# A head-mixing attention with a bilinear layer behind it: loads moved at two places, and the first chunk's scores spread over more PSUM banks

## Chip, core and metric

The kernel runs on one core of one Trainium2 chip. The metric is device time of one execution in microseconds (us). Most executions of this kernel agree within a few tenths of a per cent.

## What is computed

Inputs are drawn at random; q, k and w_pre are scaled by 8. The attention has 4 batches, 12 heads, 448 tokens and a head dimension of 64; the layer behind it has 1792 tokens, model width 768 and inner width 1536.

```python
scores = (1 / sqrt(64)) * q @ k.T                       # per batch and head
scores = einsum('bhij,hg->bgij', scores, w_pre)         # heads are mixed before ...
attn = exp(scores - max(scores)); attn /= sum(attn) + 1e-9
attn = einsum('bhij,hg->bgij', attn, w_post)            # ... and after the softmax
x = (attn @ v).transpose(0, 2, 1, 3).reshape(1792, 768)
out = ((x @ w_a) * (x @ w_b)) @ w_out
```

The weights of the layer are 64-bit numbers, which arrive as pairs of 32-bit words and are turned into float32 on the chip.

## The kernel before

**Tiling.** The queries of a batch are cut into chunks of 120, 120, 120 and 88 (16 chunks in all), and a chunk into units of 20 queries (6, 6, 6 and 5 units; 23 in a batch, 92 in all, counted from 0). Heads are kept in two groups of six, so that head i and head i + 6 make a pair.

**Steps of the attention.** `qk(c, i)` multiplies the queries of chunk c with the keys of pair i, two matmuls into a PSUM tile of two banks (tag "t", one buffer), and ScalarE copies both halves into the chunk's tile "s" (L226, L227; "s" has two buffers, so chunk c takes the place of chunk c - 2). `gather(u)` fetches a unit's rows out of "s" by four DMAs on SyncE's queue, so that head and query lie on partitions (L243, tiles "sb", buffers for four units). `premix(u)` mixes the heads by matmuls (L263, PSUM tag "m"), `smax` takes the maximum on VectorE (L272) and the exponential on ScalarE (L273), `norm` prepares the second mixing matrix on VectorE (L280 to L286), `postmix` multiplies (L296, PSUM tag "p"), `evac_p` copies the result on ScalarE (L307, tile "pt"), and `av` multiplies groups of units with v (L321, PSUM tag "x") and sends the result to DRAM (L330, L331), from where it is read as x.

**Order.** The order of all instructions is written out by hand. The loop over s runs one step for each unit: `premix(s)`, then copies of unit s - 2, `smax(s)`, the score pairs and v products that stand in a table for this step, `norm(s)`, `postmix(s - 1)`. A unit's gathers are issued three steps ahead (AH = 3). GpSimd holds loads of k, q and v for later chunks in its queue; a small copy ("tick", L121) behind each unit's sums paces them. The six pieces of v of the next batch are loaded one in each of six steps of a batch, from step V_AT on (`load_v`, L191). The six k tiles of the next batch follow between steps 12 and 16 of a batch (L195), and the first two score pairs of the next batch both stand at step 15.

**First chunk.** Ahead of the loop stand chunk 0's six pairs, 60 idle matmuls (L141), and the gathers of four units.

**Hand-over.** Once chunk 15's last score pair is placed, at step 84, the layer's first work is mixed into the last units. `load_raw` loads a weight tile of 768 KB on SyncE's queue, `load_x` one third of a batch's x, 448 KB, from DRAM (L369); x takes the buffer of chunk 14's "s". `later(fn, n)` puts an issue n steps later, ahead of that step's `premix`. `tail_ops` hands out conversions: from step 85 on, four operations at the end of each step, first six VectorE operations and one of GpSimd on the first weight (L400 to L406), then the same on the second, whose first operation (L400) is the last of step 86, then x (L375, L376). A SyncE DMA waits for the DMA eight places before it in its queue, besides its data.

Of the kernel before, what the change touches and what calls it, by code (L numbers as in the profile page):

```python
# [7 lines left out]
F32 = mybir.dt.float32  # L8
# [13 lines left out]
def talking_heads_bilinear_kernel(  # L22
# [11 lines left out]
    nc = tc.nc  # L34
    B, _, G, S = k.shape
    H, D = 2 * G, 64
# [5 lines left out]
    QG = 3  # L42
# [18 lines left out]
    WARM3 = 60  # L61
    Q1E = 3
    KL = 3
    V_AT = 9
    LQ = 4
    scale = 1.0 / float(D) ** 0.5

# [1 line left out]
    for b in range(B):  # L69
        t0 = 0  # L70
        while t0 < S:
            n = min(CHUNK, S - t0)
# [23 lines left out]
    ps = ctx.enter_context(tc.tile_pool(name="ps", bufs=2, space=PSUM))  # L96
# [28 lines left out]
    def later(fn, n=3):  # L125
        todo_at.setdefault(now[0] + n, []).append(fn)

    def setup():
        nc.vector.memset(ones, 1.0)
        nc.vector.memset(wrep, 0.0)  # L130
        for r in (0, 64):
            nc.gpsimd.dma_start(out=wrep[r:r + QH * H, 0], in_=w_pre.partition_broadcast(QH))
        for r in (0, 64):
            nc.gpsimd.dma_start(out=wrep[r:r + QH * H, 1], in_=w_post.partition_broadcast(QH))
# [8 lines left out]
    def act_table():  # L143
        nc.vector.memset(p2, 0.0)
        nc.scalar.activation(p2, p2, ACTF.Exp)
# [37 lines left out]
    kt, qraw, qt, vt = {}, {}, {}, {}  # L183
    st, sbt, mt, at, ant, ptt, pps, xps = {}, {}, {}, {}, {}, {}, {}, {}
# [8 lines left out]
    def load_k(b, i):  # L193
        t = k_p.tile([128, S], F32, tag="k", name="k")
        (nc.sync if b == 0 else nc.gpsimd).dma_start(out=t, in_=k[b, :, i])  # L195
        kt[b, i] = t
# [22 lines left out]
    def qk(c, i):  # L219
        b, t0, n = chunks[c]  # L220
        if c not in st:
            st[c] = big.tile([128, H, S], F32, tag="s", name="s")
        sp = ps.tile([128, 2, 512], F32, tag="t", name="pst", bufs=1)[:, :, :S]
        for g in range(2):
            rows = slice(D * g, D * g + D)
            nc.tensor.matmul(sp[:n, g], lhsT=qt[c, i // QG][rows, i % QG], rhs=kt[b, i][rows])  # L226
        nc.scalar.copy(st[c].rearrange("p (g i) s -> p i g s", g=2)[:n, i], sp[:n])  # L227
# [108 lines left out]
    for c in range(1, NC):  # L336
        b, t0, _ = chunks[c]
# [14 lines left out]
    for a in range(NA - 1):  # L352
        b, u0, n = groups[a]
# [11 lines left out]
    def load_x(b, parts=(0, 1, 2)):  # L365
        if b not in xt:
            xt[b] = big.tile([128, 2, KD, S], F32R, tag="s" if b < 2 else "pt", name="xhl")
        for i in parts:
            nc.sync.dma_start(out=xt[b].bitcast(F32)[:, 1, 2 * i:2 * i + 2], in_=xd[b][:, 2 * i:2 * i + 2])  # L369
# [10 lines left out]
    def load_raw(u):  # L380
        kind, i, e = u
        t = mo["c"].tile([128, CW, 2], I32, tag="raw", name="raw")
        nc.sync.dma_start(
            out=t.rearrange("p (k f) t -> p k (f t)", k=KD), in_=(w_ab if kind == "f" else w_out)[i, e].bitcast(I32)
        )
        raws[u] = t
# [106 lines left out]
    order = [("f", f, e) for f in range(3) for e in range(2)] + [("o", 0, 0), ("o", 0, 1)]  # L493
# [52 lines left out]
    with tc.manual_schedule():  # L546
        setup()
        load_q(0, 0)
        load_k(0, 0)
        load_k(0, 1)  # L550
        load_q(0, 1)
        load_k(0, 2)
        load_k(0, 3)
        act_table()
        warm_up(WARM)
        setup_mask()
        spread_q(0, 0, nc.vector)
        for i in range(G):
            if i == 1:
                spread_q(0, 1, nc.vector)  # L560
            if i + 4 < G:
                load_k(0, i + 4)
            if i == 2:
                load_q(1, 0)
                load_q(1, 1)
            qk(0, i)
        spread_q(1, 0)
        setup_w()
        nxt_g = AH + 1
        for u in range(nxt_g):  # L570
            gather(u)
        warm_up(WARM3)
        tail = iter(())

        for s in range(NU + 2):
            now[0] = s
            if s == last_prep + 1:
                open_moe()
                load_raw(order[0])
                later(lambda: load_raw(order[1]), 1)  # L580
                for i in range(3):
                    later(lambda i=i: load_x(0, (i,)), 2 + i)
                tail = tail_ops()
            if s == NU - 2:
                load_x(1)
            if s == NU - 1:
                load_x(2)
            while nxt_g <= min(s + AH, NU - 1) and ready.get(units[nxt_g][0], -1) < s:
                gather(nxt_g)
                nxt_g += 1  # L590
            pace(s - 1)
            if s in (2, 4):
                for i in range(3):
                    load_v(0, 3 * (s // 2 - 1) + i)
            b, i = divmod(s, NUB)
            if b + 1 < B and 0 <= i - V_AT < 6:
                load_v(b + 1, i - V_AT)
            for fn in todo_at.pop(s, ()):
                fn()
            if s < NU:  # L600
                premix(s)
            if s >= 2:
                for k_ in blocks_of(s - 2):
                    evac_p(k_)
            if s < NU:
                for k_ in blocks_of(s):
                    smax(k_)
            for it in items.get(s, ()):
                it[0](*it[1:])
            if s < NU:  # L610
                for k_ in blocks_of(s):
                    norm(k_)
            if 0 <= s - 1 < NU:
                for k_ in blocks_of(s - 1):
                    postmix(k_)
            for it in after.get(s, ()):
                it[0](*it[1:])
            if s >= last_prep + 2:
                take(tail, RATE if s < NU - LATE else RATE2)
            if s == NU:  # L620
                for _ in tail:
                    pass
                tail = split_ops(1)
                for k_ in blocks_of(NU - 1):
                    evac_p(k_)
                run_a(0, 0)
            if s == NU + 1:
                run_b(0, 0)
        for p in range(6):
            av(NA - 1, p)  # L630
        for t in sorted(todo_at):
            for fn in todo_at[t]:
                fn()
        todo_at.clear()
        load_x(3)
        for _ in tail:
            pass
        now[0] = 999
        late = conv_ops(range(2, 4))
        take(late, T1)  # L640
        run_a(0, 1)
        take(split_ops(2), 12)
        run_b(0, 1)
        take(late, T2)
        run_a(0, 2)
        take(late, T3)
        run_b(0, 2)
        for _ in late:
            pass
        run_a(1, 0)  # L650
        take(split_ops(3), 12)
        run_b(1, 0)
        todo = {(0, 3): order[4], (1, 1): order[5], (1, 2): order[6], (1, 3): order[7]}
        for i, u in enumerate(order[8:]):
            todo[2 + i // 3, i % 3 if u[0] == "f" else 2] = u
        nxt = 6
        pairs = [(0, 3), (1, 1), (1, 2), (1, 3)] + [(f, b) for f in range(2, KF) for b in range(B)]
        for i, (f, b) in enumerate(pairs):
            now[0] = 1000 + i
            for fn in todo_at.pop(now[0], ()):  # L660
                fn()
            if (f, b) in todo:
                ops, fin = conv(todo[f, b])
                for fn in ops:
                    fn()
                if nxt < len(order):
                    load_raw(order[nxt])
                    nxt += 1
            run_a(f, b)
            if (f, b) in todo:  # L670
                fin()
            run_b(f, b)
            if f == KF - 1 and b == 1:
                load_o(0)
                load_h(0)
                load_o(1)
                split_o(0)
            if f == KF - 1 and b > 1:
                for i in range(KF // 2 * (b - 2), KF // 2 * (b - 1)):
                    split_h(0, i)  # L680
            if b == B - 1:
                del wt["f", f]
        now[0] += 1
        for t in sorted(todo_at):
            for fn in todo_at[t]:
                fn()
        todo_at.clear()
        for j in range(B * KD):
            b, m = divmod(j, KD)
            load_o(j + 2)  # L690
            if m == 0 and b + 1 < B:
                load_h(b + 1)
            if j + 1 < B * KD:
                split_o(j + 1)
            if b + 1 < B and m >= 2:
                for f in range(3 * (m - 2), 3 * (m - 1)):
                    split_h(b + 1, f)
            run_o(j)
# [48 lines left out]
```

## Time and profile before

| | |
|---|---|
| three runs | 1010.79, 1013.9, 1014.28 us; median 1013.9 |
| profiled execution | 1010.31 us; span of its instructions 1008.6 us |
| busy share of the span | TensorE 95%, weight loads 77%, VectorE 51%, ScalarE 41%, GpSimd 29% |
| mean granted TensorE clock | 0.983 of 2.4 GHz |
| DMA | 146.6 MB moved, mean 145 GB/s |

The attention ends near 476 us of the span; the layer fills the rest and keeps TensorE busy throughout. A timeline row holds the start and the duration in us, engine, line, operation, out<-in and count; in brackets stands the idle time of the engine before it and what ended it. PE is TensorE, ACT ScalarE, DVE VectorE, POOL GpSimd, SPq the queue of SyncE.

### The profile page before, as it was taken

What the parts mean: (1) busy time and instruction counts of PE and PEld (TensorE: products, weight loads), DVE (VectorE), ACT (ScalarE), POOL (GpSimd) and SP (SyncE); (2) the same over time, 40 slices, a digit from 0 to 9 for tenths busy, and PEclk for the clock granted to TensorE, in tenths of its full rate; (3) what the DMA queues carried; (4) which work ended last, traced back from release to release, by engine and by line L of the source; (5) the groups of instructions that cost most, each with busy time, mean ns of one, the idle gap of its engine ahead of it and who ended that gap; (6) DMA issues with size and microseconds to landing.
All of it is one profiled execution on the core that took longest, in us unless ns stands there. A gap on an engine that the chain in (4) does not pass through costs nothing.

```text
span 1008.6 us, 17007 instructions
## 1 busy us (share of the span) xinstructions
PE 962.7 (95%) x6388; PEld 774.4 (77%) x6388; DVE 513.1 (51%) x1090; ACT 418.5 (41%) x854; POOL 293.0 (29%) x321
## 2 busy tenths in 40 slices
PE   7798899979999899988999999999999999999998
PEld 4465566646665566666889999999999998999997
DVE  1455355535555355567767565665555454432510
ACT  2675466756676566656321111111111133342521
POOL 2223011320123111112133323333233225555542
PEclk9999799989999899999999999999999999999999
DMA  3446233553346333348335333423333256556441
GB/s 117 156 137 199 95 123 123 156 164 97 123 136 191 104 131 119 114 155 260 112 105 188 134 118 138 146 97 139 114 139 136 85 215 244 192 202 257 146 137 68
DMA packets 63472, 146.60 MB, mean 145 GB/s; under 512 B 6252, under 2 KB 48000, under 8 KB 62368
## 3 DMA queue, kind: packets, MB, share of 16 engines
q1 hardware_dynamic: 58528, 131.11, 38.1%
q0 software_dynamic: 4864, 14.42, 5.1%
q8 instruction: 51, 0.84, 0.3%
q14 instruction: 29, 0.24, 0.1%
HBM read 80.23 MB, written 26.74 MB: 106 GB/s over the span
## 4 chain that ended last, share of the span: by engine, by line
PE 82%; DMA 11%; DVE 3%; ACT 2%; SPq 1%; issue 1%; POOL 0%; ACTq 0%; DVEq 0%
PE pp L296 13%; DMA sb<-s 10%; PE pst L226 7%; PE mp L263 7%; PE xp L321 6%; PE po L445 6%; PE po L446 6%; PE po L444 6%; PE pa L444 5%; PE pa L445 5%; PE pa L446 5%; PE pb L446 5%; PE pb L444 5%; PE pb L445 5%; ACT s L227 1%; DVE xhl L376 1%
## 5 line engine op out<-in xcount | busy, mean ns | idle before, releaser
L296 PEld LDWEIGHTS pp<-kr,a 124*112 124x112 f32 (+1 forms) x1440 | 159.7, 182 | 50.7 <-issue 33.0
L272 DVE TENSOR_REDUCE nm<-mp 124x1 f32<-124x448 f32 x180 | 104.2, 619 | 154.3 <-PE mp L263 154.3
L296 PE MATMUL pp<-kr,a 124*112 124x120 f32 (+1 forms) x1440 | 177.3, 278 | 2.8 <-ACT pt L307 1.7
L273 ACT ACTIVATE a<-mp,nm 124x448 f32<-124x448 f32 x180 | 112.7, 631 | 90.7 <-DVE nm L272 90.5
L226 PE MATMUL pst<-k,q 64*120 64x448 f32 (+1 forms) x384 | 100.1, 599 | 30.9 <-ACT s L227 30.8
L406 POOL TENSOR_TENSOR cvm<-cvm,cvr 128x768 int32<-128x768 int32 x36 | 67.0, 1860 | 211.6 <-DVE cvm L405 211.6
L434 POOL TENSOR_TENSOR wl<-rawo,wh 128x768 fp32r<-128x768 f32 x48 | 93.0, 1960 | 100.9 <-ACT wh L433 100.9
L307 ACT COPY pt<-pp 112x480 f32<-112x480 f32 x180 | 97.0, 574 | 51.7 <-PE pp L296 51.6
L456 ACT COPY sa<-pa 128x448 f32<-128x448 f32 x48 | 25.7, 536 | 221.7 <-PE pa L446 216.6
L121 POOL COPY tick<-rs 60x1 f32<-60x1 f32 x92 | 17.1, 186 | 344.9 <-DVE rs L280 344.9
L445 PE MATMUL pa<-xhl,wh 128*128 128x448 f32 x288 | 104.6, 363 | 1.9 <-DVE xhl L376 1.9
L445 PE MATMUL po<-hl,wh 128*128 128x448 f32 x288 | 104.5, 363 | 0.7 <-DVE hl L481 0.7
L444 PE MATMUL pa<-xhl,wh 128*128 128x448 f32 x288 | 104.6, 363 | 0.0
L446 PE MATMUL pa<-xhl,wl 128*128 128x448 f32 x288 | 104.4, 363 | 0.0
L444 PE MATMUL po<-hh,wh 128*128 128x448 f32 x288 | 104.4, 362 | 0.0
L446 PE MATMUL po<-hh,wl 128*128 128x448 f32 x288 | 104.4, 362 | 0.0
L446 PE MATMUL pb<-xhl,wl 128*128 128x448 f32 x282 | 102.3, 363 | 0.9 <-POOL wl L434 0.9
L226 PEld LDWEIGHTS pst<-k,q 64*120 64x120 f32 (+1 forms) x384 | 27.0, 175 | 98.5 <-ACT s L227 39.9
L444 PE MATMUL pb<-xhl,wh 128*128 128x448 f32 x282 | 102.2, 362 | 0.0
L445 PE MATMUL pb<-xhl,wh 128*128 128x448 f32 x282 | 102.2, 362 | 0.0
L227 ACT COPY s<-pst 120x896 f32<-120x896 f32 (+1 forms) x96 | 86.4, 900 | 36.6 <-PE pst L226 19.8
L263 PE MATMUL mp<-sb,wp 60*64 60x448 f32 x720 | 95.2, 564 | 3.8 <-ACT a L273 3.5
(64 smaller groups left out, 1373.1 us busy)
## 6 DMA issues: line engine op xcount, KB each, us to landing
sb<-s SPq DMA_DIRECT2D x356, 105.0 KB
raw<-in_w_ab_dram SPq DMA_DIRECT2D x24, 768.0 KB
rawo<-wod SPq DMA_DIRECT2D x24, 768.0 KB
hd<-hf SPq DMA_DIRECT2D x48, 224.0 KB
raw<-in_w_out_dram SPq DMA_DIRECT2D x12, 768.0 KB
v<-in_v_dram POOLq DMA_DIRECT2D x24, 224.0 KB, 6.0
xhl<-xd SPq DMA_DIRECT2D x12, 448.0 KB
hl<-hd SPq DMA_DIRECT2D x4, 1344.0 KB
```

What stands on the lines that cost most here:

```text
L226: nc.tensor.matmul(sp[:n, g], lhsT=qt[c, i // QG][rows, i % QG], rhs=kt[b, i][rows])
L227: nc.scalar.copy(st[c].rearrange("p (g i) s -> p i g s", g=2)[:n, i], sp[:n])
L263: nc.tensor.matmul(mt[u, i // 2][col:col + M], lhsT=wp[r:r + m, :M], rhs=tiles[i % 2][r:r + m])
L272: nc.vector.tensor_reduce(nm[:m], mp[:m], axis=AXX, op=ALU.max, negate=True)
L273: nc.scalar.activation(a[:m], mp[:m], ACTF.Exp, bias=nm[:m], scale=1.0, accum_out=rs[:m])
L296: nc.tensor.matmul(pp[:, r, :, :n], lhsT=an[:m, r * P:(r + 1) * P], rhs=kr[:m, :, :n])
L307: nc.scalar.copy(ptt[a][:P, :, :, o:o + n], pps.pop((u, j))[:, :, :, :n])
L406: lambda: nc.gpsimd.tensor_tensor(m, m, r, op=ALU.add),
L434: nc.gpsimd.tensor_tensor(ll[:, sl], raw, hh.bitcast(F32)[:, sl], op=ALU.subtract)
L444: nc.tensor.matmul(o, lhsT=hh[:, k0 + kk], rhs=mh[:, kk], start=(kk == 0), stop=False)
L445: nc.tensor.matmul(o, lhsT=hh[:, k0 + kk], rhs=ml[:, kk], start=False, stop=False)
L446: nc.tensor.matmul(o, lhsT=ll[:, k0 + kk], rhs=mh[:, kk], start=False, stop=(kk == n - 1))
```

## The change

Three edits. At the hand-over x's three parts are issued at steps 84, 85 and 87 instead of 86, 87 and 88, and the second weight at step 86 instead of 85. In chunk 0 the pairs 1, 3 and 5 no longer use the two-bank tile: each of their two halves takes a tile of one bank, of tag "m", "p" or "x", and VectorE copies it to "s". And v's pieces are loaded at steps 6 to 11 of a batch instead of 9 to 14.

```diff
-    V_AT = 9
+    V_AT = 6
...
         if c not in st:
             st[c] = big.tile([128, H, S], F32, tag="s", name="s")
+        if c == 0 and i % 2:
+            for g in range(2):
+                rows = slice(D * g, D * g + D)
+                sp = ps.tile([128, 512], F32, tag="mpx"[i // 2], name="psq")[:, :S]
+                nc.tensor.matmul(sp[:n], lhsT=qt[c, i // QG][rows, i % QG], rhs=kt[b, i][rows])
+                nc.vector.tensor_copy(st[c][:n, g * G + i], sp[:n])
+            return
         sp = ps.tile([128, 2, 512], F32, tag="t", name="pst", bufs=1)[:, :, :S]
...
                 load_raw(order[0])
-                later(lambda: load_raw(order[1]), 1)
-                for i in range(3):
-                    later(lambda i=i: load_x(0, (i,)), 2 + i)
+                load_x(0, (0,))
+                later(lambda: load_x(0, (1,)), 1)
+                later(lambda: load_raw(order[1]), 2)
+                later(lambda: load_x(0, (2,)), 3)
                 tail = tail_ops()
```

TensorE's order at the first chunk, before (pst is the two-bank tile, k the keys of a pair, q the spread queries):

```order
L226 MATMUL pst_173<-k_110,q_168 120x448 x2
L226 MATMUL pst_181<-k_112,q_168 120x448 x2
L226 MATMUL pst_189<-k_116,q_168 120x448 x2
L226 MATMUL pst_193<-k_118,q_177 120x448 x2
L226 MATMUL pst_197<-k_170,q_177 120x448 x2
L226 MATMUL pst_201<-k_179,q_177 120x448 x2
```

and after (psq is a tile of one bank):

```order
L233 MATMUL pst_173<-k_110,q_168 120x448 x2
L227 MATMUL psq_181<-k_112,q_168 120x448
L227 MATMUL psq_184<-k_112,q_168 120x448
L233 MATMUL pst_191<-k_116,q_168 120x448 x2
L227 MATMUL psq_195<-k_118,q_177 120x448
L227 MATMUL psq_198<-k_118,q_177 120x448
L233 MATMUL pst_201<-k_170,q_177 120x448 x2
L227 MATMUL psq_205<-k_179,q_177 120x448
L227 MATMUL psq_208<-k_179,q_177 120x448
```

Every second pair is now two matmuls into two tiles, which six copies on VectorE empty; they stand ahead of VectorE's set-up of the mixing matrices.

GpSimd's queue in the first batch, at the last pieces of v, before:

```order
L121 COPY tick<-rs 60x1
L191 DMA v<-in_v_dram 112x512
L195 DMA k<-in_k_dram 128x448 x2
L121 COPY tick<-rs 60x1
L191 DMA v<-in_v_dram 112x512
L202 DMA qraw<-in_q_dram 128x360
L195 DMA k<-in_k_dram 128x448
L121 COPY tick<-rs 60x1
L191 DMA v<-in_v_dram 112x512
L195 DMA k<-in_k_dram 128x448
L211 COPY q<-qraw 128x360
L121 COPY tick<-rs 60x1
```

and after, from the same place in the queue:

```order
L121 COPY tick<-rs 60x1
L191 DMA v<-in_v_dram 112x512
L202 DMA qraw<-in_q_dram 128x360
L211 COPY q<-qraw 128x3x80
L216 COPY q<-qraw 128x3x8
L121 COPY tick<-rs 60x1
L195 DMA k<-in_k_dram 128x448 x2
L121 COPY tick<-rs 60x1
L202 DMA qraw<-in_q_dram 128x360
L195 DMA k<-in_k_dram 128x448
L121 COPY tick<-rs 60x1
L195 DMA k<-in_k_dram 128x448
```

Of the three pieces of v that stood among the loads of k and q one is left, ahead of the k loads; all six now come three paces earlier.

SyncE's queue at the hand-over, before (raw is a weight tile, xhl a part of x, sb the gathers, four to a unit):

```order
L383 DMA raw<-in_w_ab_dram 128x1536
L243 DMA sb<-s 60x1x448 x8
L383 DMA raw<-in_w_ab_dram 128x1536
L243 DMA sb<-s 60x1x448 x4
L369 DMA xhl<-xd_84 128x896
L243 DMA sb<-s 60x1x448 x4
L369 DMA xhl<-xd_84 128x896
L243 DMA sb<-s 60x1x448
L243 DMA sb<-s 36x1x448
L369 DMA xhl<-xd_84 128x896
```

and after (line numbers are 7 higher there):

```order
L390 DMA raw<-in_w_ab_dram 128x1536
L376 DMA xhl<-xd_84 128x896
L250 DMA sb<-s 60x1x448 x8
L376 DMA xhl<-xd_84 128x896
L250 DMA sb<-s 60x1x448 x4
L390 DMA raw<-in_w_ab_dram 128x1536
L250 DMA sb<-s 60x1x448 x4
L376 DMA xhl<-xd_84 128x896
L250 DMA sb<-s 60x1x448
L250 DMA sb<-s 36x1x448
```

x's first part now stands right behind the first weight, its second part where the second weight stood, and the second weight where x's first part stood.

## Rows read from the trace of the kernel before

**Rows 1.** Page, parts 1 and 4: busy us and share; the chain by engine.

```profile
PE 962.7 (95%) x6388; PEld 774.4 (77%) x6388; DVE 513.1 (51%) x1090; ACT 418.5 (41%) x854; POOL 293.0 (29%) x321
...
PE 82%; DMA 11%; DVE 3%; ACT 2%; SPq 1%; issue 1%; POOL 0%; ACTq 0%; DVEq 0%
```

**Rows 2.** Timeline of the start, SyncE and TensorE.

```profile
2.67 1.87 SPq L195 DMA_DIRECT2D k<-in_k_dram  x4
...
5.51 1.03 PE L226 MATMUL pst<-k,q 64*120 64x448 f32 x4
...
7.55 1.02 PE L226 MATMUL pst<-k,q 64*120 64x448 f32 x4 [1.01 <-ACT s L227]
...
18.32 20.08 SPq L243 DMA_DIRECT2D sb<-s  x24
...
22.94 1.79 PE L263 MATMUL mp<-sb,wp 60*64 60x448 f32 x6 [0.33 <-DMA sb<-s]
```

**Rows 3.** Timeline, a chunk's first copy at four places, TensorE behind it.

```profile
71.94 0.90 ACT L227 COPY s<-pst 88x896 f32<-88x896 f32 x1 [3.62 <-DMA sb<-s]
...
104.67 0.91 ACT L227 COPY s<-pst 120x896 f32<-120x896 f32 x1 [6.59 <-DMA sb<-s]
...
105.62 1.85 PE L226 MATMUL pst<-k,q 64*120 64x448 f32 x4 [8.78 <-ACT s L227]
...
217.54 0.91 ACT L227 COPY s<-pst 120x896 f32<-120x896 f32 x1 [3.29 <-DMA sb<-s]
...
218.50 1.85 PE L226 MATMUL pst<-k,q 64*120 64x448 f32 x4 [5.49 <-ACT s L227]
...
330.28 0.91 ACT L227 COPY s<-pst 120x896 f32<-120x896 f32 x1 [3.27 <-DMA sb<-s]
```

**Rows 4.** Stretches: length, busy us (instructions) by engine, granted clock, DMA share, GB/s.

```profile
105.62:111.40 5.78, 5.78 (x24) 4.03 (x28) 0.00 (x0) 1.89 (x3) 0.00 (x0) 0.50 0.33 122
218.50:224.00 5.50, 5.50 (x24) 3.98 (x28) 0.00 (x0) 1.61 (x3) 0.00 (x0) 0.50 0.33 123
454.32:461.67 7.35, 7.35 (x57) 5.54 (x57) 7.04 (x19) 4.47 (x11) 2.49 (x2) 0.77 0.80 225
```

**Rows 5.** Timeline of the hand-over, SyncE, VectorE, TensorE and ScalarE.

```profile
444.27 0.86 SPq L383 DMA_DIRECT2D raw<-in_w_ab_dram  x1
...
448.84 1.36 SPq L369 DMA_DIRECT2D xhl<-xd  x1
...
451.85 1.05 DVE L400 TENSOR_SCALAR cvm<-raw 128x768 int32<-128x768 int32 x1 [1.31 <-DMA raw<-in_w_ab_dram]
...
452.82 1.14 DVE L272 TENSOR_REDUCE nm<-mp 124x1 f32<-124x448 f32 x2
...
454.32 1.59 PE L263 MATMUL mp<-sb,wp 60*64 60x448 f32 x8 [3.49 <-ACT a L273]
...
463.27 0.56 ACT L375 CAST xhl<-xhl 128x448 fp32r<-128x448 f32 x1 [1.65 <-DMA xhl<-xd]
...
464.35 1.89 PE L296 MATMUL pp<-kr,a 124*112 124x120 f32 x16 [1.71 <-ACT pt L307]
```

**Rows 6.** Groups by line, shapes apart: VectorE's copy of a v product from PSUM.

```profile
L330 DVE COPY xs<-xp 128x480 f32<-128x480 f32 x16 | 10.5, 657 | 21.7 <-PE xp L321 21.7
```

**Rows 7.** Timeline of GpSimd before the second boundary: a load of v.

```profile
207.05 0.55 POOL L191 DMA_DIRECT2D v<-in_v_dram  x1 [0.30 <-issue]
```

**Rows 8.** DMA queues, 196 to 217.4 us: packets, MB, share of the 16 engines.

```profile
q0 software_dynamic: 731, 2.36, 38.8%
q1 hardware_dynamic: 1696, 1.97, 30.2%
```

**Rows 9.** Chain of waits, three places: start, us, what (for a DMA, issue to landing).

```profile
63.20 8.59 DMA sb<-s
...
205.36 10.81 DMA sb<-s
...
454.02 9.23 DMA xhl<-xd
```

## The prediction

> **What bounds the kernel now.** I read the page's busy times and its chain first. TensorE is busy for 962.7 us of the 1008.6 us span, and the chain that ended last is TensorE for 82% and DMA for 11% [rows 1]. So only a few stretches can give time back: those in which TensorE stands idle or runs at a low clock. I looked for them in the timeline, and the change touches three kinds.
>
> The start [rows 2]: chunk 0's six pairs of scores share one two-bank PSUM tile. A pair takes TensorE about 1.02 us, then it waits about 1 us (1.01 us before the second pair) until ScalarE has copied the tile, which takes it 0.91 us [rows 3]. As the sixth copy ends, SyncE issues the first gather, at 18.32 us, and the first unit's matmuls at 22.94 us end a wait for a gather.
>
> The boundaries between batches [rows 3]: ScalarE's first copy of a new chunk needs the S tile of two chunks ago, which is free only when that chunk's last gather has landed. It waits 6.59 us at 104.67 and 3.29 us at 217.54; TensorE is idle 8.78 and 5.49 us. The third boundary, 3.27 us at 330.28, is like the second. After such an idle stretch the granted clock is 0.50 (1.2 GHz) for 5.78 and 5.50 us of work [rows 4], which costs half of that, 2.9 and 2.75 us.
>
> The hand-over [rows 5]: VectorE's first conversion of the second weight tile waits 1.31 us for its load; unit 87's maximum stands behind it in VectorE's order, and TensorE is idle 3.49 us. The work after it has a mean clock of 0.77 over 7.35 us [rows 4], a loss of 1.7 us. Later ScalarE waits 1.65 us for a part of x, and TensorE 1.71 us for ScalarE.
>
> **The start, part by part.** Pairs 1, 3 and 5 go to single banks that are free here, and VectorE copies them, one half at a time. TensorE no longer waits: while it runs an odd pair, ScalarE copies the even one (0.91 us, under 1.02). From 5.51 us six pairs end at about 5.51 + 6 x 1.02 = 11.6 us. No row shows VectorE copying 448 columns from PSUM here; the nearest is 480 columns in 657 ns [rows 6], so 448/480 of it, 0.61 us. Two halves take 1.2 us, within the 2.04 us of two pairs, and the last pair's two copies, from about 11.15 us, end at 12.4 us. The last of the k loads was issued by 4.54 us [rows 2] and the last pair starts at 10.6 us, so I put no wait on loads. The gathers then start at 12.4 instead of 18.32: **-5.9 us**. It goes all the way through, because the next wait is for these gathers; the 60 idle matmuls that follow the pairs and the small VectorE set-up, now behind the six copies, fit into the 4.6 us before the gathered rows arrive. Bounds: -6.7 us if ScalarE's copy decides (11.55 us), -4.5 us if a load or slower copies cost a pair's time.
>
> **v three units earlier.** No instruction is added; six 224 KB loads per batch move on GpSimd's queue, past q loads and pace copies, and GpSimd is 29% busy [rows 1]. Three of them move out of the stretch before each boundary; in the second batch these are at 196, 201 and 207 us (the last stands in [rows 7]). From 196 to 217.4 us GpSimd's queue moved 2.36 MB, the work of 10.3 such loads, in 38.8% of the engines' 21.4 us, 8.3 us or 0.81 us for each [rows 8]; the gathers were in flight for up to 10.81 us [rows 9]. If the gathers gain all of it, three loads are worth **2.4 us**; the bounds are 0 (the two queues use 69% of the engines there, so there is some room anyway) and the whole wait, 3.29 us. TensorE then idles 5.49 - 2.4 = 3.1 us. I expect the clock still to fall, as it did after 3.49 us at the hand-over, with 1.7 us lost in place of 2.75: **1.0 us** more. (Bounds: 0, and 2.75 if it stays high.) Two boundaries: **-6.8 us**, between 0 and -12.
>
> The Trainium skill (DMA: Bandwidth & Descriptors, section "Anatomy of one DMA — SWDGE (gpsimd) path") gives for the moving part bytes over 436 GB/s; as an estimate a v load is then 0.53 us and three are 1.6 us. The rows say 0.81 us for each, under contention, and a duration of the trace is used; by the page the sum would be 1.6 us smaller.
>
> At the first boundary I put **0**. There the gathers are in flight for 8.59 us already at 63 us [rows 9], and the copy at 71.94 us waits 3.62 us for them [rows 3]: the queue is behind all the way to 104 us, and all six loads come before the boundary in either order, so the last gather lands when it did. The loads at units 6 to 8 lengthen the wait at 71.94; the later wait absorbs this. Bounds: -2 (a shorter idle stretch, a shorter low clock) and +1.
>
> **The hand-over.** The four loads keep their number and bytes. x's first part goes out right behind the first weight, in time in which SyncE waits anyway; the second part takes the second weight's place (444.27 us), the second weight the first part's (448.84 us) [rows 5]. Behind each stand the gathers of the next unit on SyncE's queue. VectorE's order is unchanged, so its first conversion still stands ahead of unit 87's maximum. Before, the load was issued at 444.27 us and waited for until 451.85: 7.6 us. x parts of 448 KB took up to 9.23 us from the later places [rows 9]. The 768 KB weight now starts 4.6 us later, behind about the same bytes. With 7.6 us it lands at 456.4 us, with 9.23 us at 458.1; I take 457.2, a delay of **+5.4 us** to VectorE, to unit 87's maximum (452.82 before) and, since the matmuls at 454.32 wait for that unit's exponentials, to TensorE. Its idle stretch becomes some 9 us, like the first boundary's 8.78, so the clock costs 2.9 us instead of 1.7: **+1.2 us**. In return x's second part is long there: the 1.65 us wait of ScalarE goes, and of TensorE's 1.71 us I count **-1.0 us**, since VectorE's work for the next unit ends just behind it. Sum **+5.6 us**; bounds -2.3 us (the load lands at once, and both old waits go) and +9 (9.23 us and 1.5 us more for the larger load).
>
> **Sum.** -5.9 - 6.8 + 0 + 5.6 = -7.1 us. Against the profiled execution's own 1010.3 us that is 1003.2 us. The three runs shown lie 0.5, 3.6 and 4.0 us above the profiled one, 2.7 on average, so I predict 1003.2 + 2.7, about **1006 us**, against the median of 1013.9.
>
> **Rivals.**
>
> A. The forecast, 1002 to 1010 us: 0.58.
>
> B. The weight lands before VectorE is ready (450.5 us) or soon behind, because with x's first part early the queue is nearly empty at 448.84. For it: the first weight and x's first part go out while no gather can. Against it: the same bytes and gathers precede it as precede x's first part now. Then the hand-over costs nothing, and the sum is -12.7: 1013.0 - 12.7 = 1000.3 us, 1013.0 being the profiled time and the 2.7. 0.18.
>
> C. The boundaries stay as they are, because the gathers are held by their own pace and not by the loads (the engines are used 69%). Then the sum is -0.3: 1012.7 us. 0.13.
>
> D. The change doesn't do what it says at the start: the VectorE copies or the loads hold the pairs, or what the gathers win is lost again at the first boundary, where the queue is behind. Sum -1.2: 1011.8 us. 0.06.
>
> E. Slower: the three loads at units 6 to 8 delay the gathers of unit 11, for which the next chunk's first copy waits, in every batch as now in the first (71.94 us). It decides from the point at which 2.4 us is more than these gathers have to spare in the later batches, where no such wait stands now. Price: 2.4 us idle and 1.7 us of low clock, 4.1 us in each of three batches, and no gain at the boundaries: -5.9 + 5.6 + 12.3 = +12.0, 1025 us. 0.05.
>
> **How the numbers follow.** About 0.5% is what a measurement of this kernel can tell from no change, 5 us, so "faster" ends at 1008.8 us. A's own range crosses that; I give it three quarters faster: 0.44, with B 0.62. The rest of A, C and D make 0.33, E 0.05. The range goes from 998 (B, and a boundary at which the clock stays high) to 1013 us (C and D), which leaves out E and the far ends.
>
> **What would show it.** Right: the first gather near 12.4 us and no gap between chunk 0's pairs; waits of "s" for gathers near 1 us at the second and third boundaries and as long as before, in absolute time 6 us earlier, at the first; VectorE's first conversion of the second weight waiting 5 to 8 us, and TensorE idle some 9 us there; no wait of ScalarE for x. Wrong: that conversion waiting under 2 us (B), boundary waits of 3 us (C), new waits of a chunk's first copy at the ninth unit of the later batches (E), or six pairs that still take 2 us each (D).

## The result, and the profile after

The changed kernel takes 999.6 us (median of four runs, 996.64 to 1001.99) beside 1013.1 us for the kernel before on the same chip: a ratio of 0.988, with a 95% interval from 0.985 to 0.991. It is 1.2% faster. (The ratio is the estimate that goes with the interval; that of the two medians is 0.987.) The prediction was 1006 us, 998 to 1013.

The profiled execution of the changed kernel took 1001.99 us, the longest of its four, and its span is 1000.3 us. The one of before took 1010.31 us. The two traces are 8.3 us apart and the medians 13.5 us: the trace of before lies 2.8 us under its median, that of the changed kernel 2.4 us above. A second trace of the changed kernel, below, shows where the changed kernel's part of that lies.

The page of the changed kernel, parts 1 and 4 (as [rows 1]):

```profile
PE 960.0 (96%) x6388; PEld 772.2 (77%) x6388; DVE 518.3 (52%) x1096; ACT 416.1 (42%) x851; POOL 292.3 (29%) x321
...
PE 84%; DMA 6%; DVE 4%; ACT 2%; SPq 1%; issue 1%; POOL 0%; ACTq 0%; DVEq 0%
```

The DMAs' share of the chain fell from 11 to 6%; VectorE's rose from 3 to 4%.

The start, from the timeline of the changed kernel (as [rows 2]; L227 and L228 are the new lines for odd pairs, L233 was L226, L250 was L243):

```profile
8.17 1.02 PE L233 MATMUL pst<-k,q 64*120 64x448 f32 x4 [1.15 <-DMA k<-in_k_dram]
...
8.19 1.14 DVE L228 COPY s<-psq 120x448 f32<-120x448 f32 x2
...
13.20 11.89 SPq L250 DMA_DIRECT2D sb<-s  x15
...
17.82 1.79 PE L270 MATMUL mp<-sb,wp 60*64 60x448 f32 x6 [0.72 <-DMA sb<-s]
```

The first gather goes out at 13.20 us instead of 18.32. VectorE copies the two halves of a pair in 1.14 us. The waits of 1.0 us for ScalarE between the pairs are gone but for one of 0.24 us; one wait of 1.15 us for a load of k has come in.

The boundaries, timeline of ScalarE and TensorE in the changed kernel (as [rows 3]):

```profile
69.64 0.90 ACT L234 COPY s<-pst 88x896 f32<-88x896 f32 x1 [4.83 <-DMA sb<-s]
...
98.90 0.91 ACT L234 COPY s<-pst 120x896 f32<-120x896 f32 x1 [3.12 <-DMA sb<-s]
...
99.86 1.85 PE L233 MATMUL pst<-k,q 64*120 64x448 f32 x4 [5.32 <-ACT s L234]
...
208.74 1.38 PE L233 MATMUL pst<-k,q 64*120 64x448 f32 x4 [2.50 <-ACT s L234]
...
317.11 0.91 ACT L234 COPY s<-pst 120x896 f32<-120x896 f32 x1 [0.83 <-DMA sb<-s]
...
318.07 1.49 PE L233 MATMUL pst<-k,q 64*120 64x448 f32 x4 [3.03 <-ACT s L234]
```

TensorE's idle stretches were 8.78, 5.49 and 5.47 us; now they are 5.32, 2.50 and 3.03 us. The earlier wait in the first batch, at chunk 3's first copy, has grown from 3.62 to 4.83 us.

The stretches behind them and behind the hand-over's idle time (as [rows 4]: length, busy us and instructions of PE, PEld, DVE, ACT and POOL, granted clock, DMA share, GB/s), each as long as its counterpart of before:

```profile
99.86:105.64 5.78, 5.78 (x30) 3.54 (x32) 0.22 (x1) 2.04 (x3) 0.00 (x0) 0.69 0.32 119
208.74:214.24 5.50, 5.50 (x30) 3.65 (x32) 0.02 (x1) 2.04 (x3) 0.80 (x1) 0.69 0.52 156
318.07:323.57 5.50, 5.50 (x30) 3.55 (x32) 0.01 (x1) 2.03 (x3) 0.27 (x1) 0.69 0.47 152
446.30:453.65 7.35, 7.35 (x52) 5.07 (x53) 7.04 (x19) 4.51 (x12) 2.50 (x2) 0.64 0.43 140
```

The clock falls for a shorter time at the boundaries (0.69 instead of 0.50), and for longer at the hand-over (0.64 instead of 0.77).

The hand-over, timeline of SyncE, VectorE and TensorE in the changed kernel (as [rows 5]; L390 loads a weight, L376 a part of x):

```profile
420.78 0.36 SPq L390 DMA_DIRECT2D raw<-in_w_ab_dram  x1
421.36 0.33 SPq L376 DMA_DIRECT2D xhl<-xd  x1
...
435.86 0.96 SPq L390 DMA_DIRECT2D raw<-in_w_ab_dram  x1
...
444.03 0.56 DVE L407 TENSOR_SCALAR cvm<-raw 128x768 int32<-128x768 int32 x1 [7.57 <-DMA raw<-in_w_ab_dram]
...
446.30 2.38 PE L270 MATMUL mp<-sb,wp 60*64 60x448 f32 x8 [9.55 <-ACT a L280]
```

VectorE waits 7.57 us for the second weight instead of 1.31, and TensorE is idle 9.55 us instead of 3.49. ScalarE's wait for x is gone.

### The profile page after: what moved, and what is told of

Same layout as the page of the kernel before. It is cut to its first block, busy times and chain, and to the rows that moved or that the text cites. A ratio compares the mean times of both kernels' runs of the same rounds, so it can differ in the third digit from the quotient of the medians.

```text
span 1000.3 us, 17004 instructions
## 1 busy us (share of the span) xinstructions
PE 960.0 (96%) x6388; PEld 772.2 (77%) x6388; DVE 518.3 (52%) x1096; ACT 416.1 (42%) x851; POOL 292.3 (29%) x321
## 4 chain that ended last, share of the span: by engine, by line
PE 84%; DMA 6%; DVE 4%; ACT 2%; SPq 1%; issue 1%; POOL 0%; ACTq 0%; DVEq 0%
PE pp L303 14%; PE mp L270 7%; PE pst L233 7%; PE xp L328 7%; DMA sb<-s 6%; PE po L452 6%; PE po L453 6%; PE po L451 6%; PE pa L451 5%; PE pa L453 5%; PE pa L452 5%; PE pb L453 5%; PE pb L452 5%; PE pb L451 5%; SPq L250 1%; DVE xhl L383 1%
## 5 line engine op out<-in xcount | busy, mean ns | idle before, releaser
L279 DVE TENSOR_REDUCE nm<-mp 124x1 f32<-124x448 f32 x180 | 104.3, 620 | 131.2 <-PE mp L270 131.2
L233 PE MATMUL pst<-k,q 64*120 64x448 f32 (+1 forms) x372 | 96.4, 595 | 19.6 <-ACT s L234 18.3
L270 PE MATMUL mp<-sb,wp 60*64 60x448 f32 x720 | 96.6, 569 | 10.6 <-ACT a L280 9.8
L488 DVE TENSOR_TENSOR hl<-hl,hh 128x448 fp32r<-128x448 f32 x48 | 57.5, 1252 | 75.9 <-ACT hh L487 75.9
L234 ACT COPY s<-pst 120x896 f32<-120x896 f32 (+1 forms) x93 | 83.7, 900 | 27.3 <-PE pst L233 16.4
```

Of the source, the lines that this page charges most:

```text
L270: nc.tensor.matmul(mt[u, i // 2][col:col + M], lhsT=wp[r:r + m, :M], rhs=tiles[i % 2][r:r + m])
L279: nc.vector.tensor_reduce(nm[:m], mp[:m], axis=AXX, op=ALU.max, negate=True)
```

## The experiments

The experiments were compared with the kernel before in its own runs on the same chip, so each has a ratio. To see where the time lies, the span of each trace is cut at the first matmul of units 16 (behind the first boundary), 62 (behind the third), 87 and 91 (around the hand-over's idle stretch). These are starts of L263 or L270 in the timelines, in us, rounded to 0.1; only the first column also holds the start of the kernel. "Before + ..." is the kernel before with one part of the change or with another first unit for v; "changed + ..." is the changed kernel with another edit.

| kernel | to 16 | 16 to 62 | 62 to 87 | 87 to 91 | from 91 | ratio to before |
|---|---|---|---|---|---|---|
| before | 110.9 | 225.6 | 111.5 | 23.2 | 537.4 | 1 |
| changed | 104.3 | 218.2 | 111.4 | 29.1 | 537.3 | 0.9878 |
| changed, again | 102.5 | 215.2 | 111.5 | 28.0 | 537.3 | 0.9882 |
| before + start | 103.8 | 224.1 | 111.7 | 23.6 | 537.3 | 0.9929 |
| before + v from unit 6 | 109.6 | 215.9 | 111.5 | 23.0 | 537.5 | 0.9896 |
| before + v from unit 7 | 110.1 | 218.6 | 111.4 | 23.0 | 537.4 | 0.9943 |
| before + v from unit 8 | 108.9 | 223.2 | 111.9 | 23.0 | 537.3 | 0.9953 |
| before + hand-over | 110.7 | 223.7 | 111.7 | 27.9 | 537.3 | 1.0057 |
| changed + old hand-over | 103.7 | 215.4 | 111.5 | 23.2 | 537.4 | 0.9839 |
| changed + second weight at +1, x's first part at +0 | 102.8 | 215.3 | 111.5 | 25.0 | 537.6 | 0.9844 |
| changed + both weights at +0 | 102.4 | 215.7 | 111.4 | 22.5 | 537.5 | 0.9813 |
| changed + v from unit 15 | 97.2 | 215.2 | 111.4 | 28.8 | 537.3 | 0.9816 |
| changed + both weights at +0 + v from unit 15 | 98.9 | 215.3 | 111.8 | 21.4 | 542.9 | 0.9774 |
| the same, again | 97.8 | 216.1 | 112.1 | 21.4 | 537.5 | 0.9769 |

**The changed kernel once more.** No edit.

> The changed kernel once more, for a second trace of it. Theory (its first profiled execution was a slow one of its own: the third boundary still waited 0.83 us for the gathers and the clock fell at both later boundaries, which three kernels that share its code up to unit 84 show in at most one of the two): units 16 to 62 take 215 to 216.5 us instead of 218.2, the hand-over's conversion waits 6.5 to 8 us as before, ratio 0.986 to 0.989. Rival (the 218.2 us are what the changed kernel takes): 217.5 to 219 us.

Ratio 0.9882 (0.9862 to 0.9901). TensorE's rows at the three boundaries, timeline of this second trace, and the stretches behind the second and the third:

```profile
98.07 1.79 PE L233 MATMUL pst<-k,q 64*120 64x448 f32 x4 [2.08 <-ACT s L234]
...
206.46 1.02 PE L233 MATMUL pst<-k,q 64*120 64x448 f32 x4 [2.08 <-ACT s L234]
...
314.96 1.02 PE L233 MATMUL pst<-k,q 64*120 64x448 f32 x4 [2.17 <-ACT s L234]
```

```profile
206.46:211.96 5.50, 5.50 (x30) 3.92 (x32) 0.00 (x0) 2.03 (x3) 1.21 (x2) 0.69 0.52 158
314.96:320.46 5.50, 5.50 (x40) 3.36 (x41) 1.31 (x3) 2.95 (x6) 1.12 (x2) 1.00 0.49 161
```

Units 16 to 62 take 215.2 us and not 218.2, as the theory had it. The later boundaries wait for no gather any more; the 2.1 us left are the chunk's second pair of scores, which waits for ScalarE's copy of the first. The third boundary keeps the full clock (1.00), the second does not (0.69). So the first trace showed this kernel with less than the five other traces with v from unit six gain here (215.2 to 215.9 us).

**The start alone.** Before with the new branch for chunk 0's odd pairs:

```diff
+        if c == 0 and i % 2:
+            for g in range(2):
+                ...
+                sp = ps.tile([128, 512], F32, tag="mpx"[i // 2], name="psq")[:, :S]
+                nc.tensor.matmul(sp[:n], lhsT=..., rhs=...)
+                nc.vector.tensor_copy(st[c][:n, g * G + i], sp[:n])
+            return
```

> Before with one edit: the odd pairs of chunk 0 on single banks. Theory (the gather queue is behind throughout the first batch, so the last gather before the first boundary lands as much earlier as the first one starts): first unit 5.4 us earlier, whatever the clock loses until unit 3 is given back in a shorter wait at the first boundary (about 4 to 5 us in place of 6.59), units from 16 on 5 to 6 us earlier; all of it 5.5 us below the kernel before, ratio 0.9945. Rival (what is lost to the extra stretch at clock 0.5 stays lost, and the first boundary's gain came from v): wait at the first boundary 6.6 us as before, units from 16 on 3.5 us earlier or less, ratio 0.9965 to 0.998.

Ratio 0.9929 (0.9900 to 0.9958); unit 16 is 7.1 us earlier, where the theory had 5 to 6. Two rows of its timeline, the two waits of the first batch:

```profile
67.13 0.90 ACT L234 COPY s<-pst 88x896 f32<-88x896 f32 x1 [5.80 <-DMA sb<-s]
...
99.08 1.85 PE L233 MATMUL pst<-k,q 64*120 64x448 f32 x4 [5.40 <-ACT s L234]
```

The first wait grew (5.80 instead of 3.62 us), the second idle stretch shrank (5.40 instead of 8.78). The matmuls behind it begin at 99.08 instead of 105.62 us, 6.5 earlier; the first gather was issued at 12.70 instead of 18.32 us, 5.6 earlier. (Beside the trace of the hand-over alone, further below, which has the old start too, it is 7.3 and 6.6 us: 106.42 and 19.32 us there.) So what the start wins arrives at the boundary, wherever the work between stands still. The rival (3.5 us or less) falls.

**v alone.** Before with `V_AT = 6`.

```diff
-    V_AT = 9
+    V_AT = 6
```

> Before with one edit: v from unit six instead of nine. Theory: nothing at the first boundary (unit 16 within 0.7 us of before), 3.3 to 3.8 us at each of the second and third, together 7 us, ratio 0.993. Rival (the loads slow the gathers at the first boundary too, and moving them shortens that wait by itself): wait at the first boundary about 3 us instead of 6.59, unit 16 some 3 to 4 us earlier, together 10 to 11 us, ratio 0.99.

Ratio 0.9896 (0.9845 to 0.9947). Neither theory described the first batch rightly. Its timeline:

```profile
76.76 0.90 ACT L227 COPY s<-pst 88x896 f32<-88x896 f32 x1 [5.99 <-DMA sb<-s]
...
105.36 1.02 PE L226 MATMUL pst<-k,q 64*120 64x448 f32 x4 [2.08 <-ACT s L227]
...
213.10 0.91 ACT L227 COPY s<-pst 120x896 f32<-120x896 f32 x1 [0.22 <-DMA sb<-s]
...
322.77 1.02 PE L226 MATMUL pst<-k,q 64*120 64x448 f32 x4 [2.42 <-ACT s L227]
```

TensorE's 2.08 us at the first boundary hold no wait for gathers any more, but chunk 3's first copy waits 5.99 us instead of 3.62, and the boundary's matmuls begin at 105.36 us, where they began at 105.62 before. The wait only moved forward, to where the loads now stand. (The first gather of this trace goes out at 19.46 us, 1.1 later than in that of before, so some 1.4 us may be a gain of v.) Unit 16 comes 1.3 us earlier. At the later boundaries TensorE's idle time falls from 5.49 and 5.47 to 2.41 and 2.42 us, and units 16 to 62 take 9.7 us less. That is the total of the rival by the mechanism of the theory, with a larger price.

**Two steps between.** Before with `V_AT = 8` and with `V_AT = 7`: in each later batch one and two of the three loads leave the stretch ahead of the boundary.

> Before with v from unit eight instead of nine: in each later batch one load less in the three units ahead of the boundary. Theory (each load in that stretch costs the gathers about 0.8 us): idle stretch of TensorE at the second and third boundary 4.2 to 4.9 us (4.6 to 5.5 with three loads, 2.1 to 2.5 with none), the time 2 to 4 us below the kernel before, ratio 0.996 to 0.998. Rival (only the last load ahead of the boundary counts, or only the sum above some room): no change, ratio 0.999 to 1.001, or the whole gain, ratio 0.989 to 0.991.

> Before with v from unit seven: two loads less in the three units ahead of the later boundaries. Theory (0.8 us each): idle stretch at the second and third boundary 3 to 4 us, the time 4 to 8 us below the kernel before, ratio 0.992 to 0.996. Rival (as for the kernel with unit eight): no change, or the whole gain of v alone, ratio 0.989 to 0.991.

Ratios 0.9953 (0.9933 to 0.9974) and 0.9943 (0.9928 to 0.9959). The second boundary in the timeline of the first kernel, then of the second:

```profile
214.47 0.91 ACT L227 COPY s<-pst 120x896 f32<-120x896 f32 x1 [2.40 <-DMA sb<-s]
...
215.43 1.85 PE L226 MATMUL pst<-k,q 64*120 64x448 f32 x4 [4.59 <-ACT s L227]
```

```profile
214.50 0.91 ACT L227 COPY s<-pst 120x896 f32<-120x896 f32 x1 [1.24 <-DMA sb<-s]
...
215.45 1.61 PE L226 MATMUL pst<-k,q 64*120 64x448 f32 x4 [3.44 <-ACT s L227]
```

The same copy with all three loads there, in the timeline of the start alone, then of the hand-over alone:

```profile
209.40 0.91 ACT L234 COPY s<-pst 120x896 f32<-120x896 f32 x1 [2.48 <-DMA sb<-s]
```

```profile
216.27 0.91 ACT L227 COPY s<-pst 120x896 f32<-120x896 f32 x1 [2.44 <-DMA sb<-s]
```

With three loads there, ScalarE's wait at the second boundary is 3.29 us in the trace of before, but 2.48 and 2.44 us in these two; with two, one and none it is 2.40, 1.24 and 0.22 us. A load costs the gathers 0.7 to 1.0 us: a third of 2.44 - 0.22 or of 3.29 - 0.22. Taking the one load nearest the boundary away leaves most of the wait, so the rival of the last load falls. Whether each load counts alike is not shown: TensorE's idle time at the second and third boundary is 4.6 to 5.5 us with three loads, 4.59 and 4.37 with two, 3.44 and 2.52 with one, 2.1 to 3.0 with none, so the second step may be the larger one. The times do not tell the two kernels apart, and the first ratio shows a little more than the theory's 0.996 to 0.998.

**v behind the boundary.** The changed kernel with `V_AT = 15`: the six loads start at the boundary's own step. In the first batch the first of them goes out 3.4 us ahead of the new chunk's first copy, the other five behind it.

> The changed kernel with all six loads of v behind the boundary's first copy (from unit fifteen). Theory (in the first batch the gather queue is behind all the way and its total work up to the boundary sets when the last gather lands; a load costs it 0.8 us): six loads less before the boundary bring unit 16 by 4 to 5 us nearer, the two waits of ScalarE in that batch (4.83 and 3.12 us) fall to 2 to 3 us and to about 0.5 to 2 us; later boundaries as in the changed kernel or without their last 0.8 us; 4 to 6 us below the changed kernel, ratio 0.982 to 0.984. Rival (the first boundary is held by the gathers' own pace, v does not matter there): unit 16 within 1 us of the changed kernel, ratio 0.987 to 0.988. Second rival (the loads then hold back the gathers behind the boundary): new waits of TensorE for gathers in units 16 to 22 in each batch, ratio above 0.989.

Ratio 0.9816 (0.9780 to 0.9851). The first batch in its timeline:

```profile
66.09 0.90 ACT L234 COPY s<-pst 88x896 f32<-88x896 f32 x1 [1.44 <-DMA sb<-s]
...
94.43 1.02 PE L233 MATMUL pst<-k,q 64*120 64x448 f32 x4 [2.09 <-ACT s L234]
```

The first wait of the first batch is down to 1.44 us and that at the boundary is gone. Unit 16 comes at 97.2 us, 5.9 us ahead of the mean of the five traces of kernels with v from unit six and the new start (104.3, 102.5, 103.7, 102.8 and 102.4: 103.1 us); the two further traces with v from unit fifteen, below, have 98.9 and 97.8 us. The boundary's matmuls begin 4.2 us ahead of the same five (98.62 us on the mean), which is 0.8 us for each of the five loads behind the copy; the rest is the clock, which here stays at 1.00 behind the boundary. No new wait stands behind it. So at the first boundary the loads count, and not the gathers' own pace alone. Moving loads within the stretch ahead of it, as the change does, gains less there: with v alone from units six, seven and eight the boundary's matmuls begin at 105.36, 105.71 and 104.69 us, with the hand-over alone, whose first gather goes out as late, at 106.42 us.

**The hand-over alone**, and **the changed kernel with the old hand-over.** The same hunk forward in the kernel before and backward in the changed one:

```diff
                 load_raw(order[0])
-                later(lambda: load_raw(order[1]), 1)
-                for i in range(3):
-                    later(lambda i=i: load_x(0, (i,)), 2 + i)
+                load_x(0, (0,))
+                later(lambda: load_x(0, (1,)), 1)
+                later(lambda: load_raw(order[1]), 2)
+                later(lambda: load_x(0, (2,)), 3)
```

> Before with one edit: the new order of the hand-over's loads. Theory: VectorE's first conversion of the second weight waits 6.5 to 8 us for its load in place of 1.31, TensorE is idle 8.5 to 10 us there, ScalarE's wait of 1.65 us for x is gone; 5.8 us slower, ratio 1.0057. Rival (the long wait comes only together with the other two edits, which change what is in flight): wait of 1 to 3 us, ratio 0.998 to 1.001.

> The changed kernel with the hand-over's loads in the order of before, so the start and v alone. Theory (the three edits add up): the conversion's wait is 1.3 us and TensorE's idle stretch 3.5 us again, ScalarE waits 1.65 us for x; 5.8 us below the changed kernel, 13.5 to 19 us below the kernel before, ratio 0.982 to 0.987. Rival (the gathers, now further ahead, stand before the weight's load all the same): the wait stays at 5 to 8 us, ratio 0.988, as the changed kernel.

Ratios 1.0057 (1.0026 to 1.0089) and 0.9839 (0.9794 to 0.9885). The timeline of the hand-over alone, and below it that of the changed kernel with the old order:

```profile
455.33 0.56 DVE L400 TENSOR_SCALAR cvm<-raw 128x768 int32<-128x768 int32 x1 [6.73 <-DMA raw<-in_w_ab_dram]
...
457.32 2.38 PE L263 MATMUL mp<-sb,wp 60*64 60x448 f32 x8 [8.42 <-ACT a L273]
```

```profile
426.88 0.47 SPq L390 DMA_DIRECT2D raw<-in_w_ab_dram  x1
...
433.88 1.59 DVE L407 TENSOR_SCALAR cvm<-raw 128x768 int32<-128x768 int32 x1 [0.77 <-DMA raw<-in_w_ab_dram]
...
437.18 2.16 PE L270 MATMUL mp<-sb,wp 60*64 60x448 f32 x8 [3.77 <-ACT a L280]
```

The long wait belongs to the hand-over's new order alone, with or without the other parts, and it goes with it. Units 87 to 91 take 27.9 to 29.1 us in the four traces with the new order and 23.0 to 23.6 in the six with the old one. The three parts also add up as ratios: 0.9929 x 0.9896 x 1.0057 = 0.9882, which is the ratio of the changed kernel.

**Why the weight is late.** The changed kernel with the second weight one unit later than the first, as before, but x's first part still ahead of it; and with both weights at once, x in units two to four:

```diff
                 load_raw(order[0])
                 load_x(0, (0,))
-                later(lambda: load_x(0, (1,)), 1)
-                later(lambda: load_raw(order[1]), 2)
-                later(lambda: load_x(0, (2,)), 3)
+                later(lambda: load_raw(order[1]), 1)
+                for i in (1, 2):
+                    later(lambda i=i: load_x(0, (i,)), 1 + i)
```

> The changed kernel with the second weight one unit later than the first (its place of before), and x's first part still right behind the first weight, the other parts in units two and three. Theory (it is the weight's later place that costs): the conversion waits 1 to 2.5 us as with the old order, TensorE is idle about 3.5 us, no wait for x; 5 to 7 us below the changed kernel, ratio 0.981 to 0.984. Rival (x's first part ahead of the weight costs by its bytes and the gathers that it holds back): the wait stays at 4 to 8 us, ratio 0.986 to 0.988.

```diff
                 load_raw(order[0])
-                load_x(0, (0,))
-                later(lambda: load_x(0, (1,)), 1)
-                later(lambda: load_raw(order[1]), 2)
-                later(lambda: load_x(0, (2,)), 3)
+                load_raw(order[1])
+                for i in range(3):
+                    later(lambda i=i: load_x(0, (i,)), 2 + i)
```

> The changed kernel with the second weight right behind the first one in the first of the units, and x's three parts in units two, three and four as before. Theory (VectorE's wait is the landing of the second weight, 8 us after its issue, and VectorE asks for it some 8 us behind unit 84's issue at the earliest): no wait of the conversion above 0.5 us, TensorE's idle stretch of 9.55 us falls under 2 us, ScalarE waits up to 2 us for x; 6 to 9 us below the changed kernel, ratio to before 0.979 to 0.982, so also 2 to 3 us below the one with the old order. Rival (1.5 MB at once hold back the gathers of the next units, and TensorE waits for those instead): a wait of TensorE for gathers of 2 to 5 us, no better than the old order, ratio 0.984 to 0.988.

Ratios 0.9844 (0.9803 to 0.9884) and 0.9813 (0.9779 to 0.9847). The timeline of the first:

```profile
426.66 1.41 SPq L390 DMA_DIRECT2D raw<-in_w_ab_dram  x1
...
435.61 0.56 DVE L407 TENSOR_SCALAR cvm<-raw 128x768 int32<-128x768 int32 x1 [3.48 <-DMA raw<-in_w_ab_dram]
```

and of the second:

```profile
416.40 0.83 SPq L390 DMA_DIRECT2D raw<-in_w_ab_dram  x2
...
431.98 0.55 DVE L407 TENSOR_SCALAR cvm<-raw 128x768 int32<-128x768 int32 x1
...
434.25 1.59 PE L270 MATMUL mp<-sb,wp 60*64 60x448 f32 x8 [1.89 <-ACT a L280]
...
442.38 0.56 ACT L382 CAST xhl<-xhl 128x448 fp32r<-128x448 f32 x1 [0.83 <-DMA xhl<-xd]
```

The conversion waits 3.48 us in the first: between the theory (1 to 2.5) and the rival (4 to 8), so both have a part. The six traces with the old order have waits of 0.77 (the one above) to 2.14 us, so x's 448 KB ahead of the weight cost 1.3 to 2.7 us. The one unit more in the changed kernel, with x's second part ahead of the weight too, costs another 3.1 to 4.1 us (to 6.58 in its second trace and 7.57 in its first). With both weights at once the wait is gone, the gathers hold nothing up, and TensorE's idle stretch falls to 1.89 us. Units 87 to 91 take 22.5 us, 0.7 less than with the old order.

**Both places mended.** The two edits of `weights_first` and `v_units_15` together, and the same kernel once more:

> Both of the edits of the two kernels named weights_first and v_units_15 in the changed kernel. Theory (their places are far apart, so they add up): 10 to 15 us below the changed kernel, ratio to before 0.973 to 0.978. Rival (one of them does nothing): ratio 0.979 to 0.984.

> The kernel named weights_first_v15 once more: in its first profiled execution the work behind unit 91 took 542.9 us, while all other kernels, which have the same code there, take 537.3 to 537.6. Theory (a disturbance of that execution, nothing of the kernel): 537.3 to 537.6 us behind unit 91, units 0 to 91 as in its first trace within 2 us, profiled time 985 to 988 us, ratio to before 0.973 to 0.978. Rival (the moved loads change something in the output stage): 541 to 544 us again, ratio 0.978 to 0.981.

Ratios 0.9774 (0.9738 to 0.9810) and 0.9769 (0.9737 to 0.9800): 2.3% below the kernel before, 1.1% below the changed one, the fastest kernel of this study. Behind unit 91 its first trace took 542.9 us and its second 537.5, like all others, so nothing of the kernel did that. A stretch of the output stage in the first trace, then in the second:

```profile
830.00:980.00 150.00, 150.00 (x728) 135.72 (x727) 42.81 (x33) 56.01 (x94) 77.07 (x40) 1.00 0.48 168
```

```profile
830.00:980.00 150.00, 150.00 (x752) 140.81 (x751) 42.86 (x33) 55.94 (x94) 77.12 (x40) 1.00 0.48 169
```

TensorE got through 728 matmuls in the 150 us where it gets through 752 otherwise, with a granted clock of 1.00 in both and no wait in either.

## Why the prediction was right or wrong

Against the medians the change gained 13.5 us where the prediction had 7.1. Direction, places and signs were right; most sizes were too small on the gaining side. The median lies in the stated range, but 2.4 us below the forecast's own 1002 to 1010 us. Each term beside what the runs show (columns of the table above, means over the traces that share the code):

| term | predicted | measured |
|---|---|---|
| start and first boundary (to unit 16) | -5.9 and 0 | -7.7 (110.8 to 103.1) |
| second and third boundary (16 to 62) | -6.8 | -8.5 (224.5 to 215.95) |
| hand-over (87 to 91) | +5.6 | +5.3 (23.2 to 28.45) |
| sum | -7.1 | -10.9 |

(For 110.8: before, and before + hand-over. For 224.5: these two and before + start. For 215.95: the six traces with v from unit six. For 23.2 and 28.45: the six traces with the old order of the hand-over and the four with the new one.) The ratios 0.9878 and 0.9882 are some 12 us; the rest of about 1 us is less than two traces of one kernel differ by.

**The start: right.** The pairs no longer wait, VectorE's two copies take 1.14 to 1.16 us as estimated (1.2), and the gathers follow. The first one came at 13.20 and not 12.4 us, because a load of k held the third pair for 1.15 us, where I had put no wait: I had read when the loads were issued, not when they land. The trace of before had an early start, too: in the four other traces with the old start (the hand-over alone, v from units six, seven and eight) the first gather goes out at 19.3 to 19.5 us, not 18.32, as the clock falls among the pairs there (0.50 from 10.9 to 16.5 us with v from unit six). In the nine traces with the new start it goes out at 12.3 to 13.2. One trace could not show this. On the means of the traces in the table the first gather comes 6.0 us earlier (18.8 to 12.8 us; predicted 5.9).

**The first boundary: the mechanism was right, the 0 a little small.** That "the queue is behind all the way" and "the later wait absorbs this" is what the single edits show: with v alone the wait moves from 104 to 76 us and the matmuls of the boundary begin 0.3 us earlier; with the start alone they begin 6.5 us earlier. That the loads ahead of the boundary count, wherever they stand, is borne out by the kernel that takes five of the six behind it (unit 16 is 4.2 to 5.9 us earlier in three traces). In the first trace the wait at chunk 3's first copy grew by 1.2 us, as the text said it would; but it grew by 2.2 with the start alone, so that is no sign of the moved loads. Of the 7.7 us in the table, on the same means, 6.0 are there at the first gather, 7.4 at the boundary's matmuls (106.0 to 98.6) and the rest behind them. So the first boundary gave 1.7 us where I had 0 and a bound of -2. Only some 0.3 us of it lie behind the boundary's first matmul, where a shorter low clock would show; 1.4 us lie ahead of it, about what v alone gains there. Why loads moved within the stretch give that is not shown.

**The later boundaries: mis-sized, in the clock above all.** I had 2.4 us of idle time and 1.0 us of clock at each; the table has 8.5 us for both, 4.25 at each. TensorE's idle stretch there is 5.0 us on the mean of the three traces with v from unit nine, and 2.3 us on that of the six with v from unit six: 2.7 us less, between my 2.4 and the upper bound. The price of 0.81 us for each load, from the share of the engines' time [rows 8], lies within the 0.7 to 1.0 us that the steps show, and three loads are worth nearly the whole wait. The Trainium skill (DMA: Bandwidth & Descriptors, section "Anatomy of one DMA — SWDGE (gpsimd) path") by its bytes over 436 GB/s gives an estimate of 0.53 us; the runs do not bear that out here. The clock's part was too small: over the 5.5 us behind these boundaries the mean clock is 0.51 with v from unit nine, which loses 2.7 us. I had that fall to 1.7 us of loss at both boundaries; it does so at both in the first trace (0.69 over 5.5 us), and at only one of the two in the five others, so 1.0 us is lost on the mean and 1.7 us won. With the 2.7 us of idle time that is 4.4 us at each boundary, beside the table's 4.25.

**The hand-over: right, term by term.** The second weight is issued 15.1 us behind the first instead of 9.4, and VectorE starts on it 8.2 us behind its issue instead of 7.6; the conversion of the second weight starts 14.2 us behind that of the first instead of 8.0, which is 6.3 us later (5.3 in the second trace; predicted 5.4). TensorE's idle stretch is 9.55 and 8.56 us (predicted "some 9"), the clock is lower for longer, and the waits for x are gone. I had said that the load stands "behind about the same bytes"; that holds, since from its issue to VectorE's start it took 8.2 and 7.5 us in the two traces of the changed kernel and 7.0 to 8.4 in the six with the old order. Nearly all of the delay is the later issue, 5.7 and 5.3 us where I had 4.6.

**The rivals.** B named 1000.3 us, nearest to the median, and is wrong all the same: the weight does not land in time, and the time of that rival was met by chance, because other terms were larger. C (boundaries unchanged) falls with v alone and its steps, D with the start alone. E, a new wait in the later batches, did not come: only the first batch has it.

**The basis.** The addition of 2.7 us brought the forecast from the profiled execution to the median, and the median of before in this comparison, 1013.1 us, bears it out. It is no rule: beside the experiments the medians of before are 1009.6 to 1013.2 us. What was missing was in the terms.

## What to carry to other kernels

Here a queue that was behind for a long stretch was paid for at its end, wherever in the stretch the work beside it stood: moving loads within the stretch mostly moved the wait, moving them out removed it. A load that is wanted early should not stand behind one that is wanted later on the same queue: here the weight for which VectorE waits was put behind x, for which only ScalarE waits, and that gave back 5 us of some 16. And two traces of one kernel can differ by 3 us in the stretch in question, so a term of that size is to be read from more than one.

## What was not expected of the hardware

The granted clock after equal idle stretches is not equal: in the second trace of the changed kernel it falls behind 2.08 us of idle time at 206.46 us (1.02 us for the first pair, then a mean of 0.69 over 5.5 us), and stays at 1.00 behind 2.17 us at 314.96 us. The same holds for the start, where five of the six old pairs run at 1.02 us each in the trace of before and the sixth at 1.71 us, while they take 1.85 us from the fourth one on in three others. And the output stage of one execution ran 3% slower for some 180 us at a granted clock of 1.00 with no wait to be seen. What decides any of the three stays open.
